# First pair of heads set up ahead of the branch, and the weights' sign bit made by GpSimd, in a banded-attention and gated-MLP kernel

## The chip, the cores and the metric

The kernel runs on one core of one Trainium2 chip. The metric is the device time of one execution in microseconds; with several executions, their median.

## The reference

For a batch of 4, with 8 heads, 768 positions and 64 numbers per head, all in fp32:

```python
scores = scale * q @ k^T                                  # 768 x 768 per head
keep   = (key < n_sink) | (0 <= query - key < window)     # n_sink 4, window 128
a      = softmax(where(keep, scores, -1e9))
x      = (a @ v), heads side by side                      # 4 x 768 x 512
h      = relu(x @ w_in)                                   # 512 -> 1024
g      = sigmoid(conv of 3 taps over positions of h)
out    = (h * g) @ w_out                                  # 1024 -> 512
```

`w_in`, `conv_w` and `w_out` arrive as 64-bit floats; `n_sink` and `window` as 64-bit integers.

## The kernel before, in words

Two heads are handled as a pair, so a batch element has 4 pairs and the whole has 16. A pair has six query tiles of 128 rows. Each tile needs the scores against its own keys, the 128 keys before, and the 4 sink keys. This "banded" path holds only if the window and the sinks are small, so the kernel reads both scalars first, makes a flag (lines 874 to 876), and every engine loads it and branches (lines 904 to 913). Ahead of the branch it only starts four loads of raw q and k (line 871; pairs 0 and 1, first half), makes the identity, and the comparisons that the masks are made of (lines 895 to 902).

Behind the branch `banded` runs. `prep(0)` (line 711) transposes three 128x128 tiles of q and of k of pair 0 on TensorE (line 357), and ScalarE copies them out of PSUM (line 288), q twice with one head zeroed. VectorE makes the additive masks (lines 470 to 478, and 489 for the narrow ones of later batches); GpSimd clears two areas (493, 496). Then a loop over steps, one per query tile, issues the scores (378), and for each head one VectorE instruction that adds the mask and takes the row minimum (577), Exp with row sums on ScalarE (580), sum and reciprocal on VectorE (583, 584), the scaling on GpSimd (586). A step later the weights are transposed (603), two steps later multiplied with v (655, 678). `coming` and `prep` set up the next pairs; raw loads go into four slots that come free after each transposition (`ahead`, `fetch`).

The MLP's weights are converted in steps 2 to 18 (`WHEN`), one 128x512 tile a step, 16 in all, and the taps. A 64-bit float becomes a 32-bit one in `narrow`: ScalarE scales the high words (118), VectorE shifts that left by 3 (121), ORs in the top of the low words (122), and ORs in the sign (123). `split` then rounds to a high part on GpSimd (130) and subtracts on VectorE for the low part (131). The MLP's matmuls (`unit`: 204 and 239, with a gate on ScalarE, VectorE and GpSimd, lines 211 to 230) are cut into pieces that fill TensorE between the steps: the first third of batch 0 during steps 12 to 24, and so on; the last batch's run alone at the end.

All tiles' instructions are put in order per engine by the framework's scheduler; `follow` adds a dependency by hand that keeps one instruction behind another. Each engine runs its own in order. All loads but one output go through SP's queue.

Of the kernel before, what the change touches and what calls it, by code (L numbers as in the profile page):

```python
# [28 lines left out]
RAWB = 4  # L29
PLAIN = 4  # L30
ORDER = [("k", 0), ("k", 1), ("q", 0), ("q", 1)]
TRAIL = 2
NGB = TRAIL + 2
LA = 1
WHEN = list(range(2, 19))
AHEAD = 200


def f(ap):
    return ap.bitcast(F32)  # L40
# [26 lines left out]
class Moe:  # L67
# [206 lines left out]
class Attn:  # L274
# [12 lines left out]
    def evac(self, out, ps, scale):  # L287
        self.nc.scalar.mul(out, f(ps), scale)

# [59 lines left out]
    def prep32(self, g, half, s, kk, tag, ahead):  # L349

        c, nc, T, HTL, kw = self.c, self.nc, self.T, self.HTL, self.kw
        tiles = slice(HTL * half, HTL * half + HTL)

        def turn(nm):
            pt = self.mps.tile([P, HTL, P], F32, tag=tag, name=f"tr{nm}{g}{half}", bufs=3 if tag == "h" else 2)
            for t in range(HTL):
                c.pin(nc.tensor.transpose(pt[:, t, :], s.raw[nm, half][:, t].rearrange("p a d -> p (a d)"), c.ident))
            if nm == "q":
                s.X[half] = f(self.ap.tile([P, 2, HTL, P], F32R, tag="X", name=f"X{g}{half}", bufs=3))
                for j in range(2):  # L360
                    self.evac(s.X[half][:, j], pt, c.headscale[:, j:j + 1])
            else:
                s.kk = kk
                self.evac(kk[:, tiles, 0:P], pt, 1.0)
                if half == 0:
                    nc.scalar.copy(kk[:, :, P:kw], kk[:, 0:1, 0:kw - P].to_broadcast([P, T, kw - P]))
            ahead()

        s.plain = True
        return [lambda nm=nm: turn(nm) for nm in "qk"]  # L370

    def scores(self, s, t, pcs, lo, hi):
# [3 lines left out]
        if s.plain:  # L376
            for j, pc in enumerate(pcs):
                self.c.pin(self.nc.tensor.matmul(pc, X[:, j, u, :], kk[:, lo:hi], start=True, stop=True))
            return
# [12 lines left out]

def load(c, g, nm, t, lo, hi):

    b, hp = divmod(g, c.H // 2)
    both = getattr(c, nm)[b, 2 * hp:2 * hp + 2]
    if nm == "v" and hi - lo == c.S // P:
        c.nc.sync.dma_start(t.rearrange("p j t d -> p (j t) d"), both.rearrange("j (t p) d -> p (j t) d", p=P))
        return t
    for j in range(2):  # L400
        c.nc.sync.dma_start(t[:, j] if nm == "v" else t[:, :, j], both[j].rearrange("(t p) d -> p t d", p=P)[:, lo:hi])
    return t


def load_half(c, g, nm, half, slot):
    n = c.S // P // 2
    return load(c, g, nm, slot, n * half, n * half + n)

# [42 lines left out]
def banded(c):  # L451
# [13 lines left out]
    wide = [m.room[0][:, n:n + SW] for n in (6 * SW + T * KW, 7 * SW + T * KW)]  # L465
    m0 = cp.tile([P, P], F32, name="m0")
    m1 = cp.tile([P, KW], F32, name="m1")
    m2 = cp.tile([P, KW], F32, name="m2")
    before, sk, inw, prv = c.before, c.sk, c.inw, c.prv
# [8 lines left out]
    masks = nc.vector.tensor_scalar(w2[:, P:KW], sk[:, 0:NS], -NEG, NEG, ALU.mult, ALU.add)  # L478

# [13 lines left out]
    afterwards(nc.gpsimd.memset(A.zeros, 0.0))  # L493
    kks = [f(ap.tile([P, 4, T, KW], F32R, tag="kk", name=f"kks{i}")) for i in range(2)]
    c.vs = kks[1].rearrange("p a t k -> p (a t k)")[0:6 * SP, 2 * n0:2 * n0 + n1].rearrange("p (u n) -> p u n", u=3)
    afterwards(nc.gpsimd.memset(c.vs, 0.0))
# [18 lines left out]
    for s in st:  # L515
        s.pe, s.pT, s.sT, s.raw, s.X = {}, {}, {}, {}, [None, None]
    st[0].v = c.v_raw[0]

# [4 lines left out]
    queue += [(g, nm, None) for g in range(PLAIN, NG) for nm in "kq"]  # L523
    for i, (g, nm, half) in enumerate(queue[0:RAWB]):
        st[g].raw[nm, half] = c.raw[i]
    asked = [RAWB]

    free = [0]

    def ahead():  # L530
        free[0] += 1

    def fetch(upto=len(queue)):

        while asked[0] < min(len(queue), upto):
            g, nm, half = queue[asked[0]]
            n = 2 if half is None else 1
            if free[0] < n:
# [195 lines left out]
    for i in range(NST + DL):  # L734
        if i < NST:
# [7 lines left out]
            if g >= NPAIR or t % 3 == 2:  # L743
                fetch()
            if i == NSTB // 2:
                for x in range(0, 2 * half_row, half_row):
                    nc.sync.dma_start(f(vsr).rearrange("p u n -> p (u n)")[:, x:x + half_row], A.zeros[0:3 * SR, 0:half_row])
            if t == 0 and g and g % NPAIR == 0:
# [107 lines left out]
def attention_gated_mlp(ctx: ExitStack, tc: tile.TileContext, q, k, v, n_sink, window, w_in, conv_w, w_out, out):  # L856
# [17 lines left out]
    nc.vector.tensor_scalar(fl[:, 0:1], c.wnv, 1.0, None, ALU.is_ge)  # L874
    nc.vector.scalar_tensor_tensor(out=fl[:, 1:2], in0=c.wnv, scalar=float(P), in1=fl[:, 0:1], op0=ALU.is_le, op1=ALU.mult)
    flagged = nc.vector.scalar_tensor_tensor(out=flag, in0=c.nsv[0:1], scalar=float(NS), in1=fl[0:1, 1:2], op0=ALU.is_le, op1=ALU.mult)
    nc.scalar.activation(fl[:, 0:1], fl[:, 1:2], AF.Exp)
    c.ident = con.tile([P, P], F32, name="ident")
# [13 lines left out]
    c.before = con.tile([P, P], F32, name="before")  # L892
    wprev = con.tile([P, 1], F32, name="wprev")
# [4 lines left out]
    c.tc = tc  # L898
    follow(c, nc.vector.tensor_scalar(c.sk, C, c.nsv, None, ALU.is_lt), flagged, "flag first")
    follow(c, nc.vector.scalar_tensor_tensor(out=c.inw, in0=R, scalar=c.wnv, in1=tmp, op0=ALU.is_lt, op1=ALU.mult), flagged, "flag first")  # L900
    follow(c, nc.vector.tensor_scalar(wprev, c.wnv, -float(P), None, ALU.add), flagged, "flag first")
    nc.vector.tensor_scalar(c.prv, R, wprev, None, ALU.is_lt)
    c.pin = lambda ins: ins
# [38 lines left out]
```

## Time and profile before

| | |
|---|---|
| median of 3 runs | 475.0 us (472.65, 475.00, 475.37) |
| the profiled execution | 473.48 us |
| its span, first to last instruction | 471.8 us |
| busy share of the span: TensorE, VectorE, ScalarE, GpSimd | 94%, 72%, 68%, 60% |
| mean granted TensorE clock | 0.997 |

The time of an execution is its span and 1.7 us around it. Matmuls are pipelined and their ends modelled, so a busy TensorE is not TensorE at its peak. "PE" is TensorE's matmuls, "PEld" its weight loads, "DVE" VectorE, "ACT" ScalarE, "POOL" GpSimd, "SPq" the instructions of the queue that issues DMAs.

### The profile page before, as it was taken

How to read it: one execution, taken by the hardware profiler on the slowest of the kernel's cores; microseconds unless marked ns; L12 is line 12 of the kernel's file. 1: busy time of each engine (PE TensorE's matmuls, PEld its weight loads, DVE VectorE, ACT ScalarE, POOL GpSimd, SP SyncE). 2: the span in 40 equal slices, each digit the busy share in tenths (PEclk: the TensorE clock that was granted, in tenths of full speed). 3: DMA queues.
4: the chain of work that ended last, by engine and by line, in shares of the span. 5: the costliest groups of instructions: out<-in, count | busy, mean ns of one | idle time of the engine just before them, and what ended most of it. 6: DMA issues, size and time to landing. Idle time of an engine off the chain costs nothing.

```text
span 471.8 us, 10560 instructions
## 1 busy us (share of the span) xinstructions
PE 444.6 (94%) x3181; PEld 388.3 (82%) x3181; DVE 339.0 (72%) x1190; ACT 321.3 (68%) x1027; POOL 281.3 (60%) x557
## 2 busy tenths in 40 slices
PE   3898989898899999999999999999999999999994
PEld 3576768697798988898989898988989898998982
DVE  4799999758858668786766859685767663665562
ACT  4989957768867868785867767675857654554542
POOL 3474786626858658676755757667656671445340
PEclk9999999999999999999999999999999999999998
DMA  6888674388667472655273655545250101000001
GB/s 140 219 229 251 183 201 107 81 199 203 167 153 179 137 175 68 161 146 133 61 192 81 166 119 134 143 120 124 71 141 15 46 1 46 0 23 24 24 24 53
DMA packets 105851, 55.91 MB, mean 119 GB/s; under 512 B 83072, under 2 KB 98712, under 8 KB 105784
## 3 DMA queue, kind: packets, MB, share of 16 engines
q1 hardware_dynamic: 105640, 55.00, 45.5%
q8 instruction: 28, 0.46, 0.4%
q14 instruction: 39, 0.32, 0.2%
q10 hardware_dynamic: 144, 0.13, 0.1%
HBM read 28.17 MB, written 6.29 MB: 73 GB/s over the span
## 4 chain that ended last, share of the span: by engine, by line
PE 75%; DVE 11%; ACT 4%; POOL 3%; DMA 2%; issue 2%; DVEq 0%; POOLq 0%; ACTq 0%
PE ph L204 26%; PE po L239 25%; PE px L655 7%; PE sc L382 3%; PE sc L381 3%; PE pts L617 3%; PE px L678 2%; DVE stm L122 2%; PE tq L305 1%; PE tk L331 1%; DVE stm L123 1%; DMA kk<-bk 1%; DMA raw<-in_q_dram 1%; DVE roomH L577 1%; DVE roomL L577 1%
## 5 line engine op out<-in xcount | busy, mean ns | idle before, releaser
L239 PE MATMUL po<-woH,g 128*128 128x512 f32 x384 | 138.2, 405 | 1.5 <-POOL g L226 0.8
L204 PE MATMUL ph<-xH,wiH 128*128 128x258 f32 (+1 forms) x384 | 110.7, 288 | 0.0
L204 PE MATMUL ph<-xL,wiH 128*128 128x258 f32 (+1 forms) x384 | 109.6, 286 | 0.0
L204 PE MATMUL ph<-xH,wiL 128*128 128x258 f32 (+1 forms) x384 | 109.1, 284 | 0.0
L226 POOL TENSOR_SCALAR g<-t 128x256 fp32r<-128x256 f32 x94 | 44.3, 472 | 74.5 <-DVE t L219 50.6
L586 POOL TENSOR_SCALAR pe<-pe,sm 128x132 f32<-128x132 f32 (+1 forms) x144 | 62.8, 447 | 37.7 <-DVE sm L584 19.2
L239 PEld LDWEIGHTS po<-woH,g 128*128 128x128 f32 x384 | 69.4, 189 | 13.2 <-POOL g L226 1.7
L227 POOL TENSOR_TENSOR g<-t,g 128x256 fp32r<-128x256 f32 x94 | 74.5, 793 | 5.8
L239 PE MATMUL po<-woL,g 128*128 128x512 f32 x192 | 76.1, 396 | 0.0
L216 DVE SCALAR_TENSOR_TENSOR t<-hb,cw,t 128x256 f32<-128x256 f32 x96 | 53.8, 560 | 29.4 <-ACT t L215 28.9
L204 PEld LDWEIGHTS ph<-xH,wiL 128*128 128x128 f32 x384 | 72.8, 190 | 2.2
L204 PEld LDWEIGHTS ph<-xH,wiH 128*128 128x128 f32 x384 | 72.7, 189 | 2.0
L204 PEld LDWEIGHTS ph<-xL,wiH 128*128 128x128 f32 x384 | 72.7, 189 | 1.6
L580 ACT ACTIVATE pe<-pe,sm 128x132 f32<-128x132 f32 (+1 forms) x144 | 58.2, 406 | 14.4 <-DVE sm L577 12.8
L218 ACT ACTIVATE t<-t 128x256 f32<-128x256 f32 x96 | 40.1, 418 | 36.3 <-DVE t L217 35.9
L219 DVE SCALAR_TENSOR_TENSOR t<-t,hb 128x256 f32<-128x256 f32 x96 | 48.3, 504 | 15.1 <-ACT t L218 14.3
L215 ACT ACTIVATE t<-hb,cw 128x256 f32<-128x256 f32 x96 | 49.0, 511 | 12.4 <-POOL g L227 10.1
L217 DVE SCALAR_TENSOR_TENSOR t<-hb,cw,t 128x256 f32<-128x256 f32 x96 | 54.4, 567 | 4.0 <-POOL pe L586 0.5
L211 ACT ACTIVATE hb<-ph 128x258 f32<-128x258 f32 (+1 forms) x96 | 36.8, 384 | 17.4 <-PE ph L204 13.9
L577 DVE CUSTOM_DVE_ANT_0 pe<-sc,m 128x132 f32<-128x132 f32 (+1 forms) x144 | 39.8, 287 | 7.7 <-PE sc L382 6.9
L381 PE MATMUL sc<-kk,X 128*128 128x260 f32 (+1 forms) x144 | 42.3, 304 | 1.5 <-issue 1.1
L655 PE MATMUL px<-pT,vraw 128*64 128x128 f32 (+1 forms) x512 | 43.0, 317 | 0.0
(161 smaller groups left out, 896.1 us busy)
## 6 DMA issues: line engine op xcount, KB each, us to landing
X<-bq SPq DMA_DIRECT2D x96, 96.0 KB
vraw<-in_v_dram SPq DMA_DIRECT2D x16, 384.0 KB
out_dram<-stm SPq DMA_DIRECT2D x23, 256.0 KB
kk<-kk SPq DMA_DIRECT2D x24, 198.0 KB
raw<-in_k_dram SPq DMA_DIRECT2D x24, 192.0 KB
raw<-in_q_dram SPq DMA_DIRECT2D x24, 192.0 KB
kk<-bk SPq DMA_DIRECT2D x48, 96.0 KB
raw<-in_q_dram SPq DMA_DIRECT2D x16, 96.0 KB
```

The lines of the kernel that those rows point to most:

```text
L204: self.latest = nc.tensor.matmul(u.h[:, 0:W], w[:, cc, ff * P:(ff + 1) * P], x[:, cc, t0:t1], start=(i == 0), stop=(i == len(prods) - 1))
L215: nc.scalar.mul(a, prev, cw[:, 0, ff:ff + 1])
L216: nc.vector.scalar_tensor_tensor(out=e, in0=this, scalar=cw[:, 1, ff:ff + 1], in1=a, op0=ALU.mult, op1=ALU.add)
L217: nc.vector.scalar_tensor_tensor(out=a, in0=nxt, scalar=cw[:, 2, ff:ff + 1], in1=e, op0=ALU.mult, op1=ALU.add)
L219: nc.vector.scalar_tensor_tensor(out=a, in0=e, scalar=1.0, in1=this, op0=ALU.add, op1=ALU.mult)
L227: nc.gpsimd.tensor_tensor(out=u.g[:, 1], in0=a, in1=f(u.g[:, 0]), op=ALU.subtract)
L239: ins = nc.tensor.matmul(po[:, 0:c.DM], u.g[:, a, tt * P:(tt + 1) * P], w[:, ff, :], start=(ff == 0 and i == 0), stop=(ff == NFF - 1 and i ...
L381: self.c.pin(self.nc.tensor.matmul(pc, X[:, j, u, :], kk[:, j, lo:hi], start=True, stop=False))
L577: nc.vector.tensor_tensor_reduce(out=pe[:, j, cols], in0=pc[:, P - at:SW][:, cols], in1=mk, op0=ALU.add, op1=ALU.min, scale=1.0, scalar=3. ...
L580: exp = nc.scalar.activation(pe[:, j, cols], pe[:, j, cols], AF.Exp, bias=sm[:, j:j + 1], scale=-1.0, accum_out=sm[:, 2 + 2 * j:3 + 2 * j])
L586: nc.gpsimd.tensor_scalar(pe[:, j, cols], pe[:, j, cols], sm[:, 8 + j:9 + j], 1.0, ALU.mult, ALU.mult)
L655: ins = nc.tensor.matmul(px[h][D * j:D * j + D, P * at:P * at + n], s.v[:, j, kt, :], pT, start=(h not in open_), stop=False, skip_group_c ...
```

## The change

Ahead of the branch: the loads of k go through ScalarE's queue and those of q through SP's. A small zeroed area feeds six products whose result nobody reads (`WAKE`), then the transpositions of pair 0's k and q, then three more such products (`IDLE`). ScalarE copies the results into areas of their own (`kk0`, `X0`). GpSimd makes two of the comparisons for the masks and one of the flag; VectorE makes `m0` there. Behind the branch: GpSimd makes four strips of the masks; the narrow masks wait for a later step; four more homes for raw tiles (in a part of `kks[0]` not yet used) let pairs 2 and 3 load without waiting for a slot; v of pair 0 has its own place; the zero area is cleared at step 3, when also one key tile is copied from `kk0` to `kks[0]` by a DMA, and the sink columns by ScalarE. Pair 1's first transpositions and copies are kept behind pair 0's first scores and Exp.

In `narrow`, GpSimd writes the sign bit, `(high word < 0) * -2^31`, into the result as an integer; VectorE then does two instructions in place of three.

```diff
         first = nc.scalar.mul(low, f(hi), 2.0 ** -112)
         if len(getattr(self.c, "exps", [])) > 1:
-            follow(self.c, first, self.c.exps[-2], "late")
-        nc.vector.tensor_scalar(wi, li, 3, None, ALU.logical_shift_left)
+            follow(self.c, first, self.c.exps[-2 if len(self.c.exps) > 4 else -1], "late")
+        nc.gpsimd.tensor_scalar(wi, f(hi), 0.0, -2147483648.0, ALU.is_lt, ALU.mult)
         nc.vector.scalar_tensor_tensor(out=wi, in0=lo, scalar=29, in1=wi, op0=ALU.logical_shift_right, op1=ALU.bitwise_or)
-        nc.vector.scalar_tensor_tensor(out=wi, in0=li, scalar=-0x80000000, in1=wi, op0=ALU.bitwise_and, op1=ALU.bitwise_or)
+        nc.vector.scalar_tensor_tensor(out=wi, in0=li, scalar=3, in1=wi, op0=ALU.logical_shift_left, op1=ALU.bitwise_or)
...
-    nc.vector.tensor_tensor(out=m0, in0=inw, in1=sk, op=ALU.max)
-    nc.vector.tensor_scalar(m0, m0, -NEG, NEG, ALU.mult, ALU.add)
-    nc.vector.tensor_scalar(w1[:, KW:SW], inw, -NEG, NEG, ALU.mult, ALU.add)
-    nc.vector.tensor_scalar(w1[:, 0:P], prv, -NEG, NEG, ALU.mult, ALU.add)
+    for w in wide:
+        nc.gpsimd.tensor_scalar(w[:, 0:P], prv, -NEG, NEG, ALU.mult, ALU.add)
+        masks = nc.gpsimd.tensor_scalar(w[:, KW:SW], inw, -NEG, NEG, ALU.mult, ALU.add)
...
-    nc.vector.tensor_copy(w2, w1)
...
-            nc.vector.tensor_tensor(out=mk[:, NS:KW], in0=w[:, 0:P], in1=w[:, KW:SW], op=ALU.min)
+            ins = nc.vector.tensor_tensor(out=mk[:, NS:KW], in0=w[:, 0:P], in1=w[:, KW:SW], op=ALU.min)
+            follow(c, ins, c.turned, "late")
...
-    for x in prep(0):
-        x()
-    load_v(c, 0, 0, 0, T // 2)
+    st[0].X[0], st[0].kk, st[0].plain, st[0].v = c.X0, c.kk0, True, v0
+    for nm in "qk":
+        ahead()
     m.fetch(1)
+    fetch(RAWB + 2)
+    load(c, 0, "v", v0, 0, T // 2)
+    fetch(RAWB + 4)
+    m.fetch(2)
     sink_load(c, 0)
-    fetch()
-    m.fetch(2)
...
+        if i == T // 2:
+            follow(c, nc.gpsimd.memset(A.zeros, 0.0), c.exps[-1], "late")
+            u = T // 2 - 1
+            nc.sync.dma_start(kks[0][:, 0, u], c.kk0[:, u])
+            sinks = nc.scalar.copy(kks[0][:, 0, u + 1:T, P:KW], c.kk0[:, 0:1, 0:NS].to_broadcast([P, T - u - 1, NS]))
+            follow(c, sinks, c.exps[-1], "late")
...
-    for i in range(RAWB):
-        load_half(c, i // 2, "qk"[i % 2], 0, c.raw[i])
+    for i in range(PRE):
+        load_half(c, i // 2, "qk"[i % 2], 0, c.raw[i], nc.scalar if i % 2 else nc.sync)
+    nc.vector.memset(still, 0.0)
...
+    with tc.tile_pool(name="wake", bufs=1, space=PSUM) as wake:
+        turn = wake.tile([P, 3 * D], F32, name="turn")
+        def idle(n, last=None):
+            for i in range(n):
+                ins = nc.tensor.matmul(turn, still[:, 0:P], still, start=True, stop=True)
...
+        idle(WAKE)
+        pts = {}
+        for i, nm in ((1, "k"), (0, "q")):
+            pts[nm] = wake.tile([P, T // 2, P], F32, name=f"first{nm}")
+            for t in range(T // 2):
+                last = nc.tensor.transpose(pts[nm][:, t, :], c.raw[i][:, t].rearrange("p a d -> p (a d)"), c.ident)
+        idle(IDLE, last)
+        nc.scalar.mul(c.kk0[:, :, 0:P], pts["k"], 1.0)
+        for j in range(2):
+            nc.scalar.mul(c.X0[:, j], pts["q"], c.headscale[:, j:j + 1])
+        nc.scalar.copy(c.kk0[:, :, P:KW], c.kk0[:, 0:1, 0:NS].to_broadcast([P, T // 2, NS]))
```

## Rows read from the trace of the kernel before

**Rows 1.** The chain that ended last, summed by engine (the page).

```profile
PE 75%; DVE 11%; ACT 4%; POOL 3%; DMA 2%; issue 2%; DVEq 0%; POOLq 0%; ACTq 0%
```

**Rows 2.** Busy time of each engine by stretch: A:B us, length, then each engine.

```profile
core 0: us, PE busy (x) PEld busy (x) DVE busy (x) ACT busy (x) POOL busy (x), PEclk, DMA share, GB/s
6.90:28.00 21.10, 17.86 (x96) 13.53 (x97) 15.81 (x69) 18.43 (x60) 11.31 (x28) 1.00 0.83 212
28.00:87.00 59.00, 52.65 (x388) 42.58 (x386) 58.04 (x165) 46.25 (x135) 38.86 (x54) 1.00 0.66 181
120.00:400.00 280.00, 278.38 (x2053) 246.90 (x2052) 199.48 (x777) 196.62 (x669) 185.00 (x383) 1.00 0.46 116
```

**Rows 3.** The chain that ended last in order of time: start, us, what.

```profile
8.27 4.86 DMA raw<-in_q_dram
...
14.51 1.05 ACT X L288 x2
...
28.81 0.60 DVE stm L122
...
86.23 0.09 DVE sm L584
...
89.22 1.45 PE ph L204 x12
```

**Rows 4.** Timeline of the head: start, us, what (x: merged), idle before it.

```profile
1.25 0.42 SPq L57 DMA_DIRECT2D sc_i<-in_window_dram  x1
1.71 0.96 SPq L401 DMA_DIRECT2D raw<-in_q_dram  x2
4.79 0.17 DVE L59 CAST sc_f<-sc_i 128x4 f32<-128x4 int32 x1 [2.78 <-DMA sc_i<-in_window_dram]
5.77 0.15 DVE L876 SCALAR_TENSOR_TENSOR flag<-sc_v,fl 1x1 int32<-1x1 f32 x1
6.91 0.88 PE L357 MATMUL trq<-ident,raw 128*128 128x128 f32 x3 [6.91 <-SPq L938]
7.90 1.05 ACT L288 ACTIVATE X<-trq,headscale 128x384 f32<-128x384 f32 x2 [1.93 <-DVE roomH L474]
8.82 0.29 DVE L489 TENSOR_TENSOR m<-roomH 128x128 f32<-128x128 f32 x1
8.85 0.49 ACT L288 ACTIVATE kks<-trk 128x384 f32<-128x384 f32 x1
9.37 0.21 ACT L366 COPY kks<-kks 128x24 f32<-128x24 f32 x1
9.92 0.63 PE L378 MATMUL sc<-kks,X 128*128 128x128 f32 x2
10.71 0.29 DVE L577 CUSTOM_DVE_ANT_0 roomH<-sc,m 128x128 f32<-128x128 f32 x1 [1.60 <-PE sc L378]
15.44 0.49 PE L357 MATMUL trk<-ident,raw 128*128 128x128 f32 x3
```

**Rows 5.** VectorE's groups in the stretch 28 to 87 us: count, busy us, mean ns.

```profile
L123 DVE SCALAR_TENSOR_TENSOR stm<-stm,stm 128x512 int32<-128x512 int32 x13 | 9.7, 743 | 0.0
L121 DVE TENSOR_SCALAR stm<-stm 128x512 int32<-128x512 int32 x13 | 8.1, 620 | 0.5 <-ACT stm L118 0.3
L122 DVE SCALAR_TENSOR_TENSOR stm<-wo5r,stm 128x512 int32<-128x512 int32 x1 | 1.2, 1165 | 0.0
L122 DVE SCALAR_TENSOR_TENSOR stm<-wo0r,stm 128x512 int32<-128x512 int32 x1 | 0.7, 670 | 0.0
```

**Rows 6.** GpSimd's groups in the same stretch, with its idle time and who ended it.

```profile
L130 POOL TENSOR_SCALAR woH<-stm 128x512 fp32r<-128x512 f32 x8 | 5.2, 656 | 7.1 <-DVE stm L123 6.5 <-DVE sm L583 0.6
L227 POOL TENSOR_TENSOR g<-t,g 128x256 fp32r<-128x256 f32 x5 | 4.5, 910 | 0.4
L226 POOL TENSOR_SCALAR g<-t 128x256 fp32r<-128x256 f32 x5 | 3.3, 660 | 6.4 <-DVE t L219 6.4
```

**Rows 7.** Timeline: VectorE's line 122 and what GpSimd ran beside it.

```profile
48.41 3.75 POOL L586 TENSOR_SCALAR roomH<-roomH,sm 128x260 f32<-128x260 f32 x4
50.08 0.68 DVE L122 SCALAR_TENSOR_TENSOR stm<-wi_0r,stm 128x512 int32<-128x512 int32 x1
...
68.07 0.78 POOL L130 TENSOR_SCALAR wiH<-stm 128x512 fp32r<-128x512 f32 x1
68.30 1.09 DVE L122 SCALAR_TENSOR_TENSOR stm<-wo4r,stm 128x512 int32<-128x512 int32 x1
```

More of the change, by code (lines that the diff above doesn't have):

```diff
@@ L30 @@
 PLAIN = 4
+PRE = 4
 ORDER = [("k", 0), ("k", 1), ("q", 0), ("q", 1)]
@@ L36 @@
 AHEAD = 200
+WAKE = 6
+IDLE = 3
 def f(ap):
@@ L287, in evac @@
     def evac(self, out, ps, scale):
-        self.nc.scalar.mul(out, f(ps), scale)
+        return self.nc.scalar.mul(out, f(ps), scale)
     def pieces_of(self, name, dtype):
@@ L356, in turn @@
             for t in range(HTL):
-                c.pin(nc.tensor.transpose(pt[:, t, :], s.raw[nm, half][:, t].rearrange("p a d -> p (a d)"), c.ident))
+                ins = c.pin(nc.tensor.transpose(pt[:, t, :], s.raw[nm, half][:, t].rearrange("p a d -> p (a d)"), c.ident))
+                if g == 1 and half == 0:
+                    follow(c, ins, c.scored, "scores first")
             if nm == "q":
@@ L360, in turn @@
                 for j in range(2):
-                    self.evac(s.X[half][:, j], pt, c.headscale[:, j:j + 1])
+                    ins = self.evac(s.X[half][:, j], pt, c.headscale[:, j:j + 1])
+                    if g == 1 and half == 0:
+                        follow(c, ins, c.exps[0], "exponents first")
             else:
@@ L390, in xout, with load @@
         nc.vector.tensor_tensor(out=xL[:, hp, s], in0=px, in1=f(xH[:, hp, s]), op=ALU.subtract)
-def load(c, g, nm, t, lo, hi):
+def load(c, g, nm, t, lo, hi, by=None):
+    by = by or c.nc.sync
     b, hp = divmod(g, c.H // 2)
@@ L488, in narrow_masks @@
                                                                                 mybir.DependencyReason.DATA), reason="late")
-            nc.vector.tensor_tensor(out=mk[:, NS:KW], in0=w[:, 0:P], in1=w[:, KW:SW], op=ALU.min)
+            ins = nc.vector.tensor_tensor(out=mk[:, NS:KW], in0=w[:, 0:P], in1=w[:, KW:SW], op=ALU.min)
+            follow(c, ins, c.turned, "late")
     n0, n1 = T * KW, 3 * NPAIR * P
     A.zeros = m.room[0][:, 6 * SW:6 * SW + n0]
-    afterwards(nc.gpsimd.memset(A.zeros, 0.0))
     kks = [f(ap.tile([P, 4, T, KW], F32R, tag="kk", name=f"kks{i}")) for i in range(2)]
+    rest = kks[0].rearrange("p a t k -> p (a t k)")[:, 2 * n0:2 * n0 + 12 * P]
+    rest = [rest[:, 3 * P * i:3 * P * i + 3 * P].rearrange("p (t a d) -> p t a d", a=2, d=D) for i in range(4)]
+    homes = c.raw + rest
+    v0 = m.room[1][:, 6 * SW:6 * SW + 3 * P].rearrange("p (j t d) -> p j t d", j=2, d=D)
     c.vs = kks[1].rearrange("p a t k -> p (a t k)")[0:6 * SP, 2 * n0:2 * n0 + n1].rearrange("p (u n) -> p u n", u=3)
@@ L523, in banded @@
     queue += [(g, nm, None) for g in range(PLAIN, NG) for nm in "kq"]
[L524 to L528, printed above, removed]
+    for i, (g, nm, half) in enumerate(queue[0:PRE]):
+        st[g].raw[nm, half] = homes[i]
+    asked, turned, free = [PRE], [0], [0]
     def ahead():
-        free[0] += 1
+        free[0] += turned[0] not in range(RAWB, len(homes))
+        turned[0] += 1
     def fetch(upto=len(queue)):
@@ L536, in fetch @@
             g, nm, half = queue[asked[0]]
+            if asked[0] < len(homes):
+                st[g].raw[nm, half] = load_half(c, g, nm, half, homes[asked[0]])
+                asked[0] += 1
+                continue
             n = 2 if half is None else 1
@@ L743, in banded @@
             if g >= NPAIR or t % 3 == 2:
-                fetch()
+                fetch(2 * n + 8 if n < NPAIR else len(queue))
             if i == NSTB // 2:
                 for x in range(0, 2 * half_row, half_row):
-                    nc.sync.dma_start(f(vsr).rearrange("p u n -> p (u n)")[:, x:x + half_row], A.zeros[0:3 * SR, 0:half_row])
+                    ins = nc.sync.dma_start(f(vsr).rearrange("p u n -> p (u n)")[:, x:x + half_row], A.zeros[0:3 * SR, 0:half_row])
+                    follow(c, ins, c.exps[-1], "late")
             if t == 0 and g and g % NPAIR == 0:
@@ L869, in attention_gated_mlp @@
     c.v_raw = [con.tile([P, 2, T, D], F32, name=f"vraw{i}") for i in range(2)]
-    for i in range(RAWB):
-        load_half(c, i // 2, "qk"[i % 2], 0, c.raw[i])
+    c.X0 = c.whole[0].rearrange("p t a d -> p (t a d)").rearrange("p (a t k) -> p a t k", a=2, t=T // 2)
+    flat = c.v_raw[0].rearrange("p j t d -> p (j t d)")
+    c.kk0 = flat[:, 0:T // 2 * KW].rearrange("p (t k) -> p t k", k=KW)
+    still = flat[:, T // 2 * KW:T // 2 * KW + 3 * D]
+    for i in range(PRE):
+        load_half(c, i // 2, "qk"[i % 2], 0, c.raw[i], nc.scalar if i % 2 else nc.sync)
+    nc.vector.memset(still, 0.0)
     fl = con.tile([P, 2], F32, name="fl")
     flag = con.tile([1, 1], I32, name="flag")
[L874 to L877, printed above, removed]
+    ended = con.tile([P, 1], F32, name="ended")
+    nc.scalar.activation(ended, still[:, 0:1], AF.Exp)
+    nc.gpsimd.tensor_scalar(fl[:, 0:1], c.nsv, float(NS), None, ALU.is_le)
+    nc.vector.scalar_tensor_tensor(out=fl[:, 1:2], in0=c.wnv, scalar=float(P + 1), in1=c.wnv, op0=ALU.subtract, op1=ALU.mult)
+    flagged = nc.vector.scalar_tensor_tensor(out=flag, in0=fl[0:1, 1:2], scalar=-float(P), in1=fl[0:1, 0:1], op0=ALU.is_le, op1=ALU.mult)
     c.ident = con.tile([P, P], F32, name="ident")
@@ L897, in attention_gated_mlp @@
     nc.vector.tensor_scalar(tmp, R, 0.0, None, ALU.is_ge)
-    c.tc = tc
-    follow(c, nc.vector.tensor_scalar(c.sk, C, c.nsv, None, ALU.is_lt), flagged, "flag first")
+    c.m0 = con.tile([P, P], F32, name="m0")
+    nc.gpsimd.tensor_scalar(c.sk, C, c.nsv, 1.0, ALU.is_lt, ALU.mult)
+    nc.gpsimd.tensor_scalar(c.prv, R, c.wnv, -float(P), ALU.subtract, ALU.is_lt)
     follow(c, nc.vector.scalar_tensor_tensor(out=c.inw, in0=R, scalar=c.wnv, in1=tmp, op0=ALU.is_lt, op1=ALU.mult), flagged, "flag first")
-    follow(c, nc.vector.tensor_scalar(wprev, c.wnv, -float(P), None, ALU.add), flagged, "flag first")
-    nc.vector.tensor_scalar(c.prv, R, wprev, None, ALU.is_lt)
+    nc.vector.tensor_tensor(out=c.m0, in0=c.inw, in1=c.sk, op=ALU.max)
+    nc.vector.tensor_scalar(c.m0, c.m0, -NEG, NEG, ALU.mult, ALU.add)
+    with tc.tile_pool(name="wake", bufs=1, space=PSUM) as wake:
[3 more added lines that the diff above has]
+                ins = nc.tensor.matmul(turn, still[:, 0:P], still, start=True, stop=True)
+                if last is not None:
+                    follow(c, ins, last, "in its place")
+        idle(WAKE)
[9 more added lines that the diff above has]
+        nc.scalar.copy(c.kk0[:, :, P:KW], c.kk0[:, 0:1, 0:NS].to_broadcast([P, T // 2, NS]))
     c.pin = lambda ins: ins
```

15 lines of the change are left out of this document (6 added, 9 removed).

## The prediction

> **What bounds the kernel now.** I read the chain that ended last first. Over the whole span it is three quarters TensorE and only 11% VectorE [rows 1], which would say that VectorE is nearly worthless. That is an average over stages, so I next read busy time by stretch [rows 2]. From 120 to 400 us TensorE is busy 278.4 of 280 us: whatever ends earlier ahead of this is kept to the end. From 28 to 87 us it is VectorE that is full, 58.0 of 59 us, while TensorE, even by a measure that flatters it, is at 52.7, ScalarE at 46.3 and GpSimd at 38.9. From 6.9 to 28 us ScalarE leads with 18.4 of 21.1. The chain in order of time [rows 3] says the same: a load of raw q (8.27 us), ScalarE from 14.5 us, VectorE from 28 us until 86 us, with short pieces of GpSimd and TensorE between, and from 89 us on runs of TensorE's matmuls. So two things can be won: an earlier start of the attention, and a shorter VectorE from 28 to 87 us.
>
> **The head.** Before, the first transpositions begin at 6.91 us, behind the branch; ScalarE copies q and k out from 7.90 to 9.58 us (1.05, 0.49, 0.21), the first scores start at 9.92 and VectorE's first row minimum at 10.71 us [rows 4]. In the changed kernel this runs while the flag is being made. When can it start? The scalar of the window is issued by 1.67 us and used at 4.79 us, so 3.1 us lie between [rows 4]. The loads of q for pair 0 end their issue at 2.67 us; with the same 3.1 us q is there at 5.8 us, and k, first in ScalarE's queue, earlier. Each set of three transpositions takes 0.88 us in the head and 0.49 us at 15.44 us [rows 4]; I take the slow price, so q is done by 6.7 us. Two copies of q (1.05) and the sinks (0.21) end at 7.9 us, k's 0.49 us lies beside q's arrival. Scores then start at 7.9 instead of 9.92: a gain of 2.0 us. Bounds: 0 if the branch on ScalarE (now behind these copies) and TensorE costs what was won, since 1 us lies between the flag's end (5.92 us) and TensorE's first instruction behind the branch [rows 4]; 3.5 us if q lands sooner and the idle products have brought the products to their fast price by then (0.39 us less per set of three, and as much in the first scores). The six idle products lie in time in which TensorE did nothing (0 to 6.91 us), the three later ones beside ScalarE's copies: no cost. If the copies were not the later end, three such products would delay the scores by at most 3 x 0.3 us, an estimate from the slow set's 0.88 us for three.
>
> The rest of the head goes with it. The raw loads of pairs 2 and 3, which waited for free slots (the chain's 4.86 us from 8.27 us on [rows 3]), are now issued behind the first weight tile on SP's queue without such a wait; v of pair 0 and the sink loads move behind them, and are needed only at the first products with v, long after. So ScalarE's stretch shifts with the start and does not stay behind for a load. GpSimd's strips of the masks, and VectorE's shorter list, lie ahead of the first full-width minimum, which comes a score later. The zero area moves into step 3 on GpSimd, one clearing, and the narrow masks add two VectorE instructions of 0.29 us [rows 4] to the full stretch: 0.6 us lost.
>
> **The weights, VectorE's side.** Thirteen of the 16 shifts (line 121) lie between 28 and 87 us, 8.1 us together, 620 ns each [rows 5]. They go; lines 122 and 123 stay with the same shapes. The other three lie where ScalarE leads, so I count them as nothing. That is 8.1 us off the engine that has 1 us of idle time in this stretch.
>
> **The weights, GpSimd's side.** Thirteen new instructions of 128x512 come into the stretch. No row shows a comparison with an integer result on GpSimd. The nearest row is line 130, the same shape with two constants: 656 ns [rows 6], and I take 0.8 us for the comparison and the strided source. The other end is twice line 227's 910 ns for half the columns, 1.8 us. At 0.8 us GpSimd has 38.9 + 10.4 = 49.3 us of work for a stretch of about 53 us: it fits, tightly, since part of its idle time is waiting for VectorE's conversions (7.1 us ahead of half of line 130's, 6.4 ahead of line 226 [rows 6]), which shrinks as VectorE gets ahead. The new instruction waits for the raw tile's load and for a free buffer; queued behind it are line 586's scalings, for which the transpositions on TensorE wait. Step lags of one and two hide short waits of that kind.
>
> GpSimd also slows VectorE. Line 122 took 1.09 us beside a line 130 that ran at the same time, but 0.68 us in the middle of four of line 586 [rows 7]; its range in the stretch is 670 to 1165 ns, and line 123 has a mean of 743 [rows 5]. I put the mean loss at 0.1 us for each of some 56 instructions with two SBUF inputs in this stretch (lines 122, 123, 131, 216, 217, 219), with GpSimd busy 66% of the time. GpSimd would be busy 49.3 of 53, 93%: 0.27 / 0.66 x 0.1 x 56 = 2.3 us more. Bounds: 0 (as at 50.08 us), and 13 x 0.5 = 6.5 us, if every new instruction costs VectorE what the slowest line 122 lost against the fastest.
>
> [...]
>
> **The sum.** Head 2.0, shifts 8.1, narrow masks -0.6, contention -2.3: 7.2 us less. From the profiled execution, 473.5 us, that gives 466.3; from the median of the runs shown, 475.0, it gives 467.8. I forecast 467. By the bounds: least 0 + 8.1 - 0.6 - 6.5 = 1.0 us, most 3.5 + 8.1 - 0.6 = 11.0, and 1.5 more if the three earlier shifts count too.
>
> **The rivals.**
> 1. *The gain of the stretch is paid back* (chance 0.20). GpSimd's contention takes 6.5 us and waits of the transpositions for line 586, now later in GpSimd's queue, the last of it. Only the head stays: 473.5 - 2 = 471.5 us. For it: rows 7's slow case, and GpSimd at over 90% of the stretch. Against it: the fast case, and that TensorE and ScalarE have slack.
> 2. *GpSimd becomes the bound, and the kernel slower* (0.11). Place: 28 to 87 us. If the sign instruction takes 1.8 us, GpSimd has 38.9 + 23.4 = 62.3 us of work, and half of the 16 us in which it now waits for VectorE and TensorE stays on top: 70 us for a stretch of 59. That is 11 us more, less 2 of the head: 482.5 us. It decides from (59 + 2 - 38.9 - 8) / 13 = 1.1 us an instruction on. For it: line 227's price per column, and its place in an in-order queue ahead of line 586. Against it: line 130, of the nearest form, takes 656 ns.
> 3. *The head does not do what it says* (0.10). ScalarE reaches the branch late and loses there what the early copies won, or the products stay at their slow price. Then only the stretch stays: 473.5 - 5.2 = 468.3 us.
> 4. *Both gains come whole* (0.15). No further contention, a head of 3.5 us and all 16 shifts: 473.5 - 12.5 = 461 us.
>
> **How the numbers follow.** My forecast, 467 us with its own range of 464 to 470, has 0.44. About 1%, 4.75 us, is what a measurement of this kernel can tell from no change; the bound for faster is 470.2. Faster: nearly all of the forecast (0.41), rival 4 (0.15), most of rival 3 (0.07), a little of rival 1 (0.02): 0.65. Slower: rival 2, 0.11. Within 1%: the rest, 0.24. The range reaches down past rival 4's middle, to 458.5, and up past rival 1, to 476, leaving out most of rival 2 and the outer part of rival 4, under 2 in 10.
>
> **What would show it.** In the changed profile line 121's successor stands on GpSimd, 16 times, near 0.8 us: over 1.1 speaks for rival 2. VectorE's first row minimum should start near 8.7 us instead of 10.7; later than 10 speaks for rival 3. The stretch in which VectorE is full should end near 80 us instead of 87. Lines 122 and 123 with means over 0.95 us speak for rival 1, as do longer waits of line 603 for line 586. From 120 us on nothing should differ but the shift. The forecast is wrong if the stretch ends where it did, or if TensorE shows new idle time behind it.

## The result, and the profile after

The changed kernel takes 480.8 us (median of 5 runs, 479.58 to 481.67) against 475.4 us before: a ratio of 1.0127, with a 95% interval of 1.0095 to 1.016. It is slower by 1.3%; the prediction had 467 us. The profiled execution has a span of 479.0 us, 7.2 us more than before. In the changed file the new sign instruction is L124, the two instructions left on VectorE are L125 and L126, the high part on GpSimd L133, the low part on VectorE L134, the softmax scaling on GpSimd L597, and the row minimum L588.

The chain that ended last, by engine, to be laid beside [rows 1]:

```profile
PE 71%; POOL 10%; DVE 7%; ACT 3%; DMA 2%; issue 2%; POOLq 0%; DVEq 0%; ACTq 0%
```

GpSimd went from 3% to 10% of the chain and VectorE from 11% to 7%. The busy time by stretch says where, beside [rows 2]:

```profile
core 0: us, PE busy (x) PEld busy (x) DVE busy (x) ACT busy (x) POOL busy (x), PEclk, DMA share, GB/s
6.90:28.00 21.10, 16.70 (x97) 12.34 (x96) 13.38 (x57) 16.97 (x56) 18.57 (x40) 0.92 0.74 195
28.00:87.00 59.00, 53.79 (x396) 43.52 (x395) 49.98 (x152) 48.06 (x143) 54.39 (x65) 1.00 0.64 175
120.00:400.00 280.00, 277.95 (x2052) 246.08 (x2051) 202.64 (x797) 198.67 (x680) 187.08 (x391) 1.00 0.47 118
```

From 28 to 87 us VectorE's busy time fell by 8.1 us. That this equals the shifts' 8.1 of [rows 5] is chance: fewer conversions pass through the stretch, and some of their instructions got longer, as the groups below show. GpSimd rose from 38.9 to 54.4 us and is now the fullest engine, in the head too (18.6 of 21.1 us). From 120 us on TensorE is full in both kernels. The groups of the stretch (last columns: count, busy us, mean ns, idle before it):

```profile
L124 POOL TENSOR_SCALAR stm<-wi_3r 128x512 int32<-128x512 f32 x2 | 4.0, 2022 | 0.0
...
L125 DVE SCALAR_TENSOR_TENSOR stm<-wo4r,stm 128x512 int32<-128x512 int32 x1 | 0.9, 948 | 0.0
...
L126 DVE SCALAR_TENSOR_TENSOR stm<-stm,stm 128x512 int32<-128x512 int32 x11 | 8.9, 812 | 0.1
...
L134 DVE TENSOR_TENSOR wiL<-stm,wiH 128x512 fp32r<-128x512 f32 x6 | 6.3, 1053 | 3.8 <-POOL wiH L133 3.6
L134 DVE TENSOR_TENSOR woL<-stm,woH 128x512 fp32r<-128x512 f32 x4 | 4.4, 1102 | 0.7 <-POOL woH L133 0.7
```

In the same stretch of the kernel before, the low part was:

```profile
L131 DVE TENSOR_TENSOR woL<-stm,woH 128x512 fp32r<-128x512 f32 x8 | 5.6, 696 | 0.0
L131 DVE TENSOR_TENSOR wiL<-stm,wiH 128x512 fp32r<-128x512 f32 x6 | 4.3, 719 | 0.0
```

The sign instruction takes 2 us, not 0.8. Only 10 conversions finish in the stretch instead of 14 (the counts of L134 and L131). And the low part, which has two SBUF inputs, went from 0.71 to 1.07 us beside a GpSimd that is busy 54.4 of the 59 us. The last low part of all starts at 107.4 us instead of 86.6. The chain in order of time (start, us, what) shows GpSimd's place in it:

```profile
59.31 1.97 POOL stm L124
61.28 0.59 POOL roomL L597
...
82.62 1.96 POOL stm L124
84.58 0.47 POOL roomL L597
...
88.11 1.97 POOL stm L124
90.08 2.50 POOL roomL L597 x2
...
101.43 0.55 PE tk L334 x3
```

At each of these three places the sign instruction stands ahead of a softmax scaling in GpSimd's in-order queue. TensorE's transpositions, which need the scaled weights, do not wait longer for them than before, though. What TensorE's matmuls waited for (us in total, times, longest us), first in this kernel, then in the kernel before:

```profile
PE pts L614 <- POOL roomL L597: 1.4, 2, 1.0
PE pt L614 <- POOL roomL L597: 0.7, 1, 0.7
```

```profile
PE pts L603 <- POOL roomL L586: 1.8, 3, 0.8
PE pts L603 <- POOL roomH L586: 1.4, 3, 0.6
PE pt L603 <- POOL roomL L586: 0.9, 1, 0.9
```

That is 2.1 us against 4.1. Where the chain goes on from these scalings is other work: the MLP's gate on GpSimd (L229, from 62.87 and from 92.58 us on) and VectorE's next conversion (L125, at 85.10 us). The chain is TensorE's from 101 us on, where it was from 89 [rows 3].

The head did come earlier. TensorE's and VectorE's timelines, beside [rows 4]:

```profile
6.66 0.52 PE L943 MATMUL firstq<-ident,raw 128*128 128x128 f32 x3 [0.39 <-DMA raw<-in_q_dram]
...
8.00 0.87 PE L385 MATMUL sc<-vraw,raw 128*128 128x128 f32 x4
```

```profile
9.13 0.29 DVE L588 CUSTOM_DVE_ANT_0 roomH<-sc,m 128x128 f32<-128x128 f32 x1 [0.58 <-POOL sm L511]
```

The first scores start at 8.00 instead of 9.92 us, the first row minimum at 9.13 instead of 10.71, held for its last piece by a clearing in GpSimd's queue.

### The profile page after: what moved, and what is told of

The parts are those of the page before. It is cut to its first block, busy times and chain, and to the rows that moved or that the text cites. A ratio compares the mean times of both kernels' runs of the same rounds, so it can differ in the third digit from the quotient of the medians.

```text
span 479.0 us, 10608 instructions
## 1 busy us (share of the span) xinstructions
PE 454.2 (95%) x3199; PEld 393.7 (82%) x3199; DVE 336.3 (70%) x1167; ACT 322.7 (67%) x1028; POOL 313.8 (66%) x581
## 4 chain that ended last, share of the span: by engine, by line
PE 71%; POOL 10%; DVE 7%; ACT 3%; DMA 2%; issue 2%; POOLq 0%; DVEq 0%; ACTq 0%
PE ph L207 25%; PE po L242 25%; PE px L666 7%; PE pts L628 3%; PE sc L389 3%; PE sc L388 3%; POOL roomL L597 2%; PE px L689 2%; POOL stm L124 2%; POOL roomH L597 1%; PE tk L334 1%; PE tq L308 1%; DMA kks<-in_q_dram 1%; DMA kk<-bk 1%; POOL g L229 1%
## 5 line engine op out<-in xcount | busy, mean ns | idle before, releaser
L597 POOL TENSOR_SCALAR pe<-pe,sm 128x132 f32<-128x132 f32 (+1 forms) x144 | 61.8, 441 | 37.8 <-DVE sm L595 26.6
L229 POOL TENSOR_SCALAR g<-t 128x256 fp32r<-128x256 f32 x94 | 45.0, 479 | 61.9 <-DVE t L222 41.3
L219 DVE SCALAR_TENSOR_TENSOR t<-hb,cw,t 128x256 f32<-128x256 f32 x96 | 52.8, 550 | 35.5 <-ACT t L218 35.0
L220 DVE SCALAR_TENSOR_TENSOR t<-hb,cw,t 128x256 f32<-128x256 f32 x96 | 53.4, 557 | 3.5
L632 POOL TENSOR_SCALAR_AFFINE_SELECT pT<-pT 128x256 f32<-128x256 f32 x60 | 27.7, 461 | 28.9 <-ACT pT L630 27.6
L588 DVE CUSTOM_DVE_ANT_0 pe<-sc,m 128x132 f32<-128x132 f32 (+1 forms) x144 | 39.4, 285 | 4.1 <-PE sc L389 3.7
```

The source lines that it names most:

```text
L219: nc.vector.scalar_tensor_tensor(out=e, in0=this, scalar=cw[:, 1, ff:ff + 1], in1=a, op0=ALU.mult, op1=ALU.add)
L220: nc.vector.scalar_tensor_tensor(out=a, in0=nxt, scalar=cw[:, 2, ff:ff + 1], in1=e, op0=ALU.mult, op1=ALU.add)
L229: nc.gpsimd.tensor_scalar(u.g[:, 0], a, 1.0, 1.0, ALU.mult, ALU.mult)
L597: nc.gpsimd.tensor_scalar(pe[:, j, cols], pe[:, j, cols], sm[:, 8 + j:9 + j], 1.0, ALU.mult, ALU.mult)
```

## The experiments

Every time stands beside runs of the kernel before on the same chip; the ratios carry the comparison.

**What the sign instruction costs by itself.** A small kernel of loose instructions, with no attention and no MLP in it.

> Prices of forms on an idle core: one raw weight tile is loaded, each form runs three times on it, and the outputs are filled with zeros; nothing of attention or the MLP is computed. On GpSimd, 128x512: the changed kernel's sign instruction (strided source, comparison and product, integer result); the same from a contiguous source; the same with an fp32 result; comparison from a contiguous source with an fp32 result; two products from the strided source; two products with an integer result; and line 130's two products. Theory A says nothing on which part is dear. If the integer result is dear, the forms with it take near 2 us and those without near 0.6; if the comparison is dear, the forms with it; if the strided source, those. On VectorE the mask of the sign bit from the strided source should take 0.4 to 0.6 us.

Its timeline (L91 and L94 are the comparison from strided and from contiguous columns, L100 and L106 a product with two constants):

```profile
24.59 1.94 POOL L91 TENSOR_SCALAR signF<-raw 128x512 int32<-128x512 f32 x1
...
28.40 0.64 POOL L100 TENSOR_SCALAR mulf<-raw 128x512 f32<-128x512 f32 x1
29.01 1.92 POOL L94 TENSOR_SCALAR contig<-flat 128x512 int32<-128x512 f32 x1
...
31.48 0.61 POOL L106 TENSOR_SCALAR ref<-flat 128x512 f32<-128x512 f32 x1
32.06 1.92 POOL L109 TENSOR_SCALAR contigf<-flat 128x512 f32<-128x512 f32 x1
```

The stride and the type of the result (L109 writes floats) change at most 0.03 us; the shape is the same in all. The comparison in place of a multiplication changes 1.3 us. VectorE makes the same comparison, on the same columns, in 0.41 us at best, and in 0.84 and 0.86 us the two other times, with GpSimd busy beside all three:

```profile
6.79 0.41 DVE L115 TENSOR_SCALAR dvesign<-raw 128x512 int32<-128x512 f32 x1
...
7.86 0.84 DVE L115 TENSOR_SCALAR dvesign<-raw 128x512 int32<-128x512 f32 x1
```

**The two parts apart.** In the first run the changed narrow gets its three VectorE instructions back; in the second the kernel before gets the change's three lines there.

```
e1:  -  nc.gpsimd.tensor_scalar(wi, f(hi), 0.0, -2147483648.0, ALU.is_lt, ALU.mult)
     +  nc.vector.tensor_scalar(wi, li, 3, None, ALU.logical_shift_left)
        ...
```

> The changed kernel with the three VectorE instructions of before in the weights' conversion: the head alone. Theory A (the sign instruction's 1.97 us on GpSimd, 16 times, is the whole loss): the first row minimum stays at 9.1 us, 1.6 us earlier than before, VectorE is full again from about 26 us on, GpSimd has idle time, and the time is about 2 us under before, 472 to 474 us. Rival B (edits of the head cost later too, through the order of the loads, the zero area, or TensorE's lower granted clock between 20 and 30 us): 477 us or more, with a granted clock under 1.00 in that stretch again. Rival C (work on GpSimd is paid back by VectorE whatever its price): the same as theory A here.

> The kernel before with only the sign bit moved to GpSimd: nothing of the head. Theory A: 16 x 1.97 us make GpSimd full from about 20 to 95 us, and the time is the changed kernel's without its head's 1.6 us, 482 to 483 us. Rival B: the sign edit is not where the loss lies, so about 475 us or less. Rival C: as theory A.

Head alone: 478.7 us, ratio 1.0074 (1.0047 to 1.0101). Sign alone: 483.3 us, 1.019 (1.0129 to 1.0251). Both parts lose by themselves. The sign's loss was foreseen by the price; that of the head needs a cause of its own. Together they lose 1.27%, less than the sum.

**The sign made cheap.** In the next two runs GpSimd makes the sign bit as the high word times zero (-0.0 for a negative word), at the price of a product: 0.61 to 0.64 us in p_prices, where the comparison took 1.92 to 1.94.

```
-  nc.gpsimd.tensor_scalar(wi, f(hi), 0.0, -2147483648.0, ALU.is_lt, ALU.mult)
+  nc.gpsimd.tensor_scalar(w, f(hi), 0.0, 1.0, ALU.mult, ALU.mult)
```

> The changed kernel whole, but GpSimd makes the sign bit as the high word times 0.0 (a product that is -0.0 for negative numbers, whose only bit is the sign), in fp32, in the form of line 130 in the kernel before (0.62 us). Theory A: the instruction takes 0.6 to 0.9 us, GpSimd has idle time again, VectorE keeps the 8 us it was relieved of, less some contention: 465 to 470 us. Rival B: the loss stays with the head, 473 us or more. Rival C (VectorE's instructions with two SBUF inputs lose what GpSimd gains, since line 134 took 1.13 us instead of 0.69 beside GpSimd): line 134 stays over 1 us and the time is within 2 us of the kernel before.

> The kernel before with the conversions' sign bit made on GpSimd as a product with zero (0.6 us each beside 1.95 for the comparison) and two instructions left on VectorE; nothing of the head is changed. Theory A (VectorE is what the stretch from 28 to 87 us waits for, so a mask taken off it at a low price is a gain): 466 to 471 us, and the conversions end by 82 us instead of 87. Rival C (GpSimd, which the stretch also fills, and the slower two-input instructions beside it pay the mask back): 474 to 477 us. Rival D (a conversion is a chain of one instruction behind another, over a third engine, and the crossing costs more than the mask saved): 478 us or more.

In the changed kernel: 480.35 us, 1.0103 (1.0052 to 1.0153), not to be told from the comparison's 1.0127. In the kernel before, with no head edit: 479.15 us, 1.0094 (1.006 to 1.0128). The products take 0.64 to 1.06 us in the first run and 0.64 to 0.82 in the second. So a mask taken off the full engine, at about the price that the prediction had used, on an engine with 20 us to spare, makes the kernel slower. The price of the comparison can't be all of it.

**Single edits of the head.** The first frees the two zero transfers into vsr from the Exp behind which they stand; the second takes out all the ordering edits; the third the idle products (WAKE and IDLE 0).

> The head part alone (478.7 us) without the order that holds the two zero transfers into vsr behind an Exp. Theory L (loads: what stands in SyncE's queue ahead of the weights makes ScalarE wait for them, 2.8 us for wi_1r at 50 us): the two transfers go back to before 40 us, wi_1r is issued by 44 us, and the time falls by 1 to 3 us, to 475.5 to 477.7. Rival K (TensorE's granted clock, 0.50 in two stretches of 3.4 us that the kernel before does not have, is what costs): 478 to 479.5 us. Rival G (masks, memsets and scalings on GpSimd): 478 to 479.5 us.

> The head part alone without any of its ordering edits: the zero transfers and the second pair's first transposes and evictions are held by nothing, the conversions' scaling follows the last but one Exp from the start as before, and q and k are asked for as early as before. Theory L (the order of loads and of queues): 472 to 475 us, with no wait of ScalarE for a weight load above 1 us. Rival K (the clock): 477 to 480 us, with at least two stretches at a granted clock of 0.50 before 60 us. Rival G (work moved to GpSimd and the copied first keys): 477 to 480 us with GpSimd the releaser of more of the chain than before.

> The head part alone with no idle products at all. Theory L: the first transposes take twice as long, the first row minimum comes 0.5 to 1.5 us later, and the end 0 to 1.5 us later, 478.5 to 480.2 us. Rival K (idle products raise the granted clock early and the chip takes it back between 25 and 45 us): the low stretches move and the time falls by 1 us or more, to 477.5 us or less.

477.9 us (1.0058, 1.0038 to 1.0078), 483.4 us (1.0161, 1.0119 to 1.0203) and 476.7 us (1.0045, 1.0026 to 1.0064). In the second, loads asked for without the bound can land on the first pair's scaled q before its scores, so some scores are of other queries; only its time is read. Late loads (theory L) were right in one place: in the head kernel ScalarE's in-order queue stands still for a weight, 2.77 us.

```profile
52.81 0.67 ACT L121 ACTIVATE stm<-wi_1r 128x512 f32<-128x512 f32 x1 [2.77 <-DMA wi_1r<-in_moe_w_in_dram]
```

But against the head's 1.0074 the first gave back 0.0016 and the third 0.0029 (0.8 and 1.4 us), with intervals that overlap the head's, and undoing all the ordering cost 0.0087 (4.1 us) more. None of the three is the cause by itself. The third came out where rival K had it, at 477.5 us or less, but not by fewer slow stretches: TensorE's granted clock is under 0.80 in six stretches of 2 us ahead of 120 us, in the head kernel in four.

**Is it the order of the queues?** The framework's planner places every instruction in its engine's queue by its own estimate of when it will be ready, so any edit can move all that stands behind it. The listing of the zero-product kernel of e5 against the kernel before bears this out: TensorE's queues part at the 34th matmul, ScalarE's at the 16th instruction. The next runs hold the queues by edges that order two instructions of one engine and wait for nothing.

```
+  for engine, names in ORDERS.items():
+      ...
+          c.tc.add_manual_dep(ins, last.name, mybir.DependencyInfo(mybir.DependencyClass.NoSync, ...), reason="order")
```

> The kernel before, instruction for instruction, with its queues held in the order that the planner gave to the zero-product kernel. Theory O: 477 to 481 us, as that kernel. Rival D: within 1% of the kernel before, 471 to 477 us.

> The zero-product sign on GpSimd again (479.2 us when the planner was free), but with the queues of TensorE, ScalarE, VectorE, GpSimd and SyncE held in the order that they have in the kernel before; only the new GpSimd instruction is placed freely. Theory O (the planner orders every queue anew for any edit, from its own estimates, and the order of the kernel before is worth what the edits lost): 466 to 473 us, conversions ended by 84 us. Rival D (the crossing to a third engine, or contention, is what costs, whatever the order): 477 us or more.

> The change's own sign instruction (a comparison, 1.95 us on GpSimd) in the kernel before, with the queues held in the order of the kernel before. With the planner free it took 483.3 us. If the price of the comparison is all of that loss, 482 to 485 us here too. Theory O: the order is the part that this run takes away, and 16 comparisons at 1.95 us on a GpSimd that has some 6 us of room between 28 and 87 us leave 475 to 480 us.

> The kernel before with one number of its planner's priorities changed (150 for 200), which alters no instruction, only their order in the queues. Theory O, if most orders are worse than the one of the kernel before: 477 to 484 us. If the planner's orders are all alike to the chip: 472 to 477 us.

The kernel before, instruction for instruction, in the other's order (its 17 shifts, which the other kernel lacks, stay where the planner puts them): 477.35 us, 1.0093 (1.0066 to 1.012). That is the whole 1.0094 of e5, with no instruction changed. The kernel before was not run with such edges in its own order; that they cost little by themselves is read from e14 below, which carries about as many. A milder reordering (n_ahead150): 475.3 us, 1.0037 (1.0022 to 1.0052): a time in the range expected if all orders were alike, but a ratio clear of 1. So order alone is worth some 4 us in e12, as theory O had it. But its other half fell: the cheap sign in the old order takes 477.7 us, 1.0093 (1.0073 to 1.0113), as much as in the new one, and the dear sign in the old order 492.3 us, 1.0393 (1.0369 to 1.0417), above both of its expectations. The planner's new order is not an accident beside the edit. It gave back some 9 of the 18 us that the dear instruction costs in the old one. The transpositions show one place: from 6.9 to 110 us TensorE's matmuls waited 12.2 us for the scalings in the old order (e13), 2.6 us in the new one (e2), and 4.1 us in the kernel before.

The cheap sign in the old order shows how even 0.8 us on GpSimd is paid. GpSimd's and TensorE's timelines (in this file L282 is the sign, L291 the high part, L747 the scaling, L764 the transpositions):

```profile
53.87 0.62 POOL L291 TENSOR_SCALAR wiH<-stm 128x512 fp32r<-128x512 f32 x1
54.46 0.81 POOL L282 TENSOR_SCALAR stm<-wi_1r 128x512 f32<-128x512 f32 x1
55.26 2.12 POOL L747 TENSOR_SCALAR roomH<-roomH,sm 128x260 f32<-128x260 f32 x2
```

```profile
56.22 0.33 PE L764 MATMUL pts<-ident,roomH 128*128 128x128 f32 x1 [1.20 <-POOL roomH L747]
57.43 0.84 PE L764 MATMUL pts<-ident,roomH 128*128 128x128 f32 x3 [0.88 <-POOL roomH L747]
```

And the stretches of 2 us around it (columns as in [rows 2]):

```profile
54.00:56.00 2.00, 1.03 (x6) 0.62 (x6) 2.00 (x3) 1.58 (x6) 2.00 (x3) 1.00 0.19 68
56.00:58.00 2.00, 0.90 (x4) 0.71 (x5) 2.00 (x9) 0.60 (x2) 1.92 (x4) 0.89 0.00 0
58.00:60.00 2.00, 2.00 (x12) 1.99 (x11) 0.67 (x2) 2.00 (x7) 2.00 (x3) 0.50 0.77 254
60.00:62.00 2.00, 2.00 (x12) 1.89 (x12) 0.10 (x1) 1.60 (x5) 1.31 (x3) 0.76 0.02 8
```

High part and sign go ahead of two scalings; TensorE stands for 2.1 us; its granted clock then falls from 1.00 to 0.50, and is back at 1.00 from 62 us on. The order being held, the same matmuls can be laid side by side: twelve of the MLP's products and three transpositions, up to the scores behind them, first here, then in the kernel before at a granted clock of 1.00.

```profile
58.13 0.56 PE L365 MATMUL ph<-xH,wiH 128*128 128x258 f32 x1
...
61.27 0.60 PE L539 MATMUL sc<-kks,X 128*128 128x260 f32 x2
```

```profile
55.11 0.37 PE L204 MATMUL ph<-xH,wiH 128*128 128x258 f32 x1
...
56.97 0.60 PE L378 MATMUL sc<-kks,X 128*128 128x260 f32 x2
```

They take 3.14 us instead of 1.86. Ahead of the wait this kernel is 1.0 us behind the kernel before (the scores at 54.42 and 53.42 us), behind the wait 3.0, and behind the slow stretch 4.3. So 2.0 us went with the wait and 1.3 with the clock at this place; the whole span is 3.8 us longer. VectorE, the engine that was to be relieved, is busy 0.77 of the 4 us from 58 on, and its timeline names what it waits for:

```profile
61.90 0.43 DVE L738 CUSTOM_DVE_ANT_0 roomL<-sc,roomH 128x260 f32<-128x260 f32 x1 [3.24 <-PE sc L539]
```

Here 2.1 us of waiting were followed by a stretch at a granted clock of 0.50, and VectorE, full in the kernel before, stood for 3.24 us.

**The head in the old order.** The same edges, for the instructions that the head kernel has in common with the kernel before (over 5,400), from about the second pair on.

> The head part alone (478.7 us), with the queues of all five engines held, from about the second pair on, in the order that the kernel before has for the same instructions. Theory O (the head's lead of 1.6 us at the first row minimum and 3.4 us at the first pair's products is lost because the planner orders everything behind it anew): 471 to 474.5 us, with the first pairs' products at or ahead of the times of the kernel before. Rival L2 (the head's own edits, its loads and its work on GpSimd, cost more than they bring, whatever the order): 476 us or more.

> The same, with the order held on TensorE, ScalarE, VectorE and GpSimd alone: SyncE's queue of loads is the planner's. Theory L (late loads of weights are what loses the lead): 2 us or more above the run that holds the loads too, and ScalarE waits over 1 us for a weight load. Otherwise within 1 us of it.

> The head part in the old order and without its idle products. If the idle products bring what they are for (the first transposes at the higher clock): 0.5 to 1.5 us above the run with them. If they cost (the granted clock falls later): 1 us or more below it.

474.6 us, 1.0008 (0.9992 to 1.0024); with SyncE's loads left to the planner 475.9 us, 1.002 (1.0 to 1.004); without idle products 475.5 us, 1.0022 (1.0004 to 1.004). The order of the queues is the head's whole loss: with it held, 1.0074 becomes 1.0008. The loads' order and the idle products can't be told from nothing here. But the head's lead is not cashed either. TensorE's timelines say why: first this kernel (L518 transposes q), then the same transpositions in the kernel before.

```profile
15.36 0.52 PE L518 MATMUL trq<-ident,kks 128*128 128x128 f32 x3 [1.46 <-DMA kks<-in_q_dram]
```

```profile
13.60 0.88 PE L357 MATMUL trq<-ident,raw 128*128 128x128 f32 x3 [0.38 <-DMA kks<-in_v_dram]
```

The head began 1.9 us earlier and is 1.8 us later here. The load of the third pair's q is issued at 8.92 us, behind two tiles of weights and v; in the kernel before at 8.27 [rows 3]. The last run issues it first.

> The head part in the old order, with the third pair's q and k asked for as SyncE's first loads behind the branch (ahead of two weight loads and v). If that load is what takes the head's lead: it lands by 13 us, TensorE's wait of 1.5 us at 15.4 us goes, and the time falls by 1 to 2 us, to 472.5 to 473.8 us, under the kernel before. Rival (the lead is lost later all the same, to the load that is now late or to the granted clock): within 0.8 us of 474.6 us.

475.5 us, 1.0027 (1.0006 to 1.0048): no gain. The timeline of TensorE:

```profile
11.88 0.49 PE L518 MATMUL trq<-ident,kks 128*128 128x128 f32 x3
...
17.04 0.52 PE L518 MATMUL trq<-ident,kks 128*128 128x128 f32 x3 [1.84 <-DMA kks<-in_v_dram]
```

The wait for the third pair's q is gone, 3.5 us earlier, and a longer one stands at the fourth's, whose load this queue issues at 11.01 us (the releaser is inferred and names the tile that both share). The chain then goes over two weight loads:

```profile
18.89 4.68 DMA wi_2r<-in_moe_w_in_dram
...
28.12 3.85 DMA wo0r<-in_moe_w_out_dram
```

From 9.5 to 18.6 us, ahead of them, it is ScalarE's. On this chain ScalarE's work and the row of loads bound the head, not the start of the first pair. That is read from the chain; no run brought all the loads earlier.

## Why the prediction was wrong

Two steps failed. The first is the price of the new instruction, "line 130, the same shape with two constants: 656 ns ..., and I take 0.8 us". It measured 1.95 to 2.13 us, past the 1.1 us that the prediction had named as the mark of rival 2. The lower bound was a multiplication, and at one and the same shape the operation made the price on GpSimd: 1.92 us against 0.61 in p_prices.

The second step decides, for with the price near 0.8 us the changed kernel still takes 480.35 us (e4); only without the head edits is the dear price worth some 1% (1.019 in e2 against 1.0094 in e5). It is "8.1 us off the engine that has 1 us of idle time": busy time taken off VectorE was counted as time off the kernel. By the sum the shifts less their contention gain 5.8 us; alone, at the cheap price, they cost 0.94% (e5). The head's term failed in the same way: 2.0 us less the 0.6 for the narrow masks by the sum, a loss of 0.74% alone (e1). What the runs showed in its place are queues: scalings that stand behind new work on GpSimd while TensorE waits (2.1 us at the place in e11, 12.2 us in all in e13) and then slows (to a granted clock of 0.50 in both), and an order of all the queues that the edits change (e12, e14).

Rival 2 had 0.11 and came out at 482.5 us; measured were 480.8. The other end of the price, 1.8 us, was the better number, and two rows with a ratio of nearly three between them, where no row showed the operation, deserved more than that. Of its mechanism the changed kernel shows a part: GpSimd is the fullest engine, and the scalings stand behind the sign instruction. The transpositions' wait for them did not grow there (2.1 us against 4.1); it did in the old order (12.2 us, e13). And e4 is as slow without the dear price. So that rival 2 came so near in microseconds is in part luck.

The shifts: the 8.1 us came out to 0.1 us as busy time by chance, with 10 conversions finished in the stretch instead of 14, and were worth nothing as time (e5).

Contention: the forecast had 0.1 us for each of 56 instructions beside a GpSimd that is fuller, and 2.3 us more in all. What was shown is uneven. L134 lost 0.36 us a piece (1.07 against 0.71), 3.6 us for its ten; L126 lost 0.07 against line 123 [rows 5], 0.8 us for eleven. L125 did not lose (0.77 against 0.80 for line 122), and the gate's L219 and L220 got shorter (0.49 and 0.48 us against 0.71 and 0.67). Over the six lines that the prediction names it comes to some 2.6 us for 43 instructions. So the total was met, but by luck: it lies on other instructions than an even price puts it on.

That the instructions with two SBUF inputs are the ones that lose was the author's assumption, and no run shows it. L125 has two such inputs, as L134 has, and did not lose. VectorE's comparison in p_prices, with one input, took 0.41 us once and 0.84 and 0.86 us the two other times, each beside a busy GpSimd.

The head: "a gain of 2.0 us" at the first scores was right (1.92), 1.6 at the first row minimum, where a clearing on GpSimd was the later end. The idle products did bring the fast price (0.52 us for q's three; 0.87 without them, in e16). Wrong was the step behind it, "ScalarE's stretch shifts with the start and does not stay behind for a load". I took the loads' queue for free because the slots were; but the third pair's q went behind two weight tiles and v, at 8.93 us in the changed kernel, and e14 and e17 show TensorE waiting for the third or the fourth pair's q. Rival 3 asked whether the head does what it says; at its start it did, and was then held up by something that neither the forecast nor the rival priced.

Not in the prediction at all was the order of the queues. It added and removed instructions in a fixed order. Here the order was worth 0.93% by itself, some 4.4 us without any instruction changed (e12): twice the head's 2.0 us, and over half of the shifts' 8.1.

The sum 1.0074 and 1.019 against 1.0127 isn't explained piece by piece. Why the planner's order for the head kernel is slow, which of its thousand moves does it, was not tried; nor was the clock held up in one of these kernels, so how much of the loss the half-clock stretches are, beside the waits ahead of them, stays open outside the one place of e11. In the changed kernel the stretches of 2 us with a lower granted clock are 22 to 28 us (0.85, 0.50, 0.80) and 88 to 92 us (0.56, 0.58). If each costs its length times what its clock lacks to 1.00, they are 3.4 us of the 7.2; that is an estimate, an upper one for TensorE's own work, since it also waits in them, and without what other engines lose behind it. They are not the measure of the loss: e4 has four such stretches ahead of 90 us and takes as long as the changed kernel with two, and in e9 the same estimate gives 5.1 us, more than twice its loss of 0.45%.

## What to carry to other kernels

Price an instruction by a row with the same operation on the same engine (a product took 0.61 us here and a comparison 1.92); where there is none, measure it alone first, and give the dear end its share of the chance. Before moving work off the full engine, see whether what queues behind it on the other engine is what the bottleneck waits for, as the scalings were for 2.1 us at the place in e11: read that queue, not its busy share. And where a planner orders the queues, hold the order to learn what an edit costs, and run the old instructions in the new order to learn what the order costs.

## What the runs showed of the hardware

In p_prices a 128x512 comparison with a multiplication on GpSimd took 1.92 to 1.94 us, two multiplications 0.61 to 0.64 us, both where VectorE was idle beside them, with strided or contiguous columns, floats or integers out.

In the profiled execution TensorE's granted clock, by stretches of 2 us, dropped to 0.50 or 0.51 somewhere in the first 120 us in 13 of the 16 kernels run beside the kernel before; in that one it was 1.00 in all of them. In e11 it came behind 4 us in which TensorE was busy 1.93 us. A pair's 20 products on the chain of waits, in such a stretch of e1 and at the full clock in e11:

```profile
29.56 2.33 PE px L666 x20
```

```profile
38.27 1.24 PE px L816 x20
```
